# A recurrence and a two-layer network in FP32: the second group's second layer in three passes, a pair of blocks begun one group later

## The chip, the cores and the metric

The kernel runs on one core of a Trainium2 chip. A core has engines that run side by side, each with an instruction queue of its own: TensorE (PE: matrix products, with weight loads as a queue beside them), VectorE (DVE), ScalarE (ACT), GpSimd (POOL), and SyncE (SP), which here issues every DMA transfer. The metric is the device time of one execution in microseconds (us), as a median of several runs.

## The reference: what is computed

First a gated recurrence, for 4 batches and 8 heads of 48 numbers over 768 steps:

```
state = alpha[t][:, None] * state + outer(k[t], v[t])
y[t]  = q[t] @ state
```

Then y, seen as x of 3072 tokens by 384 numbers, goes through a network with two weight matrices (384 x 2048 and 2048 x 384):

```
h = max(x @ w_in, 0);  out = (h * h) @ w_out
```

All results are FP32.

## The kernel before

**Attention.** The 3072 tokens are 24 blocks of 128. A block's recurrence is computed by sums of logs (`cs`, lines 297 to 301), exponentials of them that scale q and k, transposes (`turn`, line 590, tile T), products of scores and state sums (`sckv`, lines 432 and 460), a masked copy (`am`, line 443), a new state (`us` and `s`, lines 473, 489, 490; the last factor comes by a DMA round trip, `last<-row`, line 344) and the outputs (`y`, line 412), which ScalarE copies into x (line 628). Blocks are taken in pairs, named by the first block: pair 12 is blocks 12 and 13. The function `attention` lists a pair's steps with due times. A call begins one pair (`n0`) and, with `after`, also finishes the pair before it; then the products sckv of the new pair and y of the old one share two interruptions of the network's products (`ga` and `gb`).

**Network.** Four blocks make a group, six groups in all (g = 0 to 5; the text calls g = 1 the second group and g = 2 the third). The weights are eight pieces per matrix, and a piece makes two of the sixteen 128-wide tiles of h. The first group uses true FP32 products ("plain"). From the second on a number is split into a near part a (or b for a weight), a rest l and a difference d, and a product of two numbers becomes three single passes: near by near, rest by rest, difference by difference. The first layer is `in_x` (the first two passes) and `in_y` (the third, two tiles later), line 737; `in_post` squares the result. The second layer is `out_x` and `out_y`, both through `of_tile`, line 820. In the second layer the first group has six plain pieces (`out_plain`) and two in three passes, the second group four and four (k1 = 4), and the others have all eight in three passes.

**Splits.** `split_h` makes ha on ScalarE (line 710) and hl on VectorE (line 660), `diff_h` makes hd on VectorE (line 714). The weights are prepared once, in the first and second group: `cast_w` (line 665, ScalarE), `rest_w` (line 660, VectorE), `scale_w` (line 679, ScalarE) and `diff_w` (line 660, VectorE). Rests and differences are stored to DRAM (`keep`, line 670) and read again for each later group (`pump`, line 703). `pump` reads ahead only while the number of pieces held is under `room`. The near parts stay.

**Order of work.** The network's steps are units with planned costs (1.05 for `in_x`, 1.08 for `out_x`). Everything else is an event with a due time in the same units, and `weave` puts the events between the units; each engine then runs its instructions in that order. All due times are in the table `AT`. `align` (line 1018) is an event too: it pads TensorE's instruction stream with NOPs up to a given offset within 256 instructions; `pads` gives group, time and offset, and `places` the pair ahead of whose transposes one stands.

Of the kernel before, what the change touches and what calls it, by code (L numbers as in the profile page):

```python
# [18 lines left out]
AT = {'v_by': (2.5, 3.5, 5.0), 'before': 2.2, 'places': ((4, 203), (16, 188)), 'pads': ((1, 33.0, 218), (2, 0.5, 83), (2, 5.5, 178)), 'evs': 0.65, 'lead': 4, 'post': 3, 'w_first': (45.25, 42.0, 55.95), 'wstep': 1.6, 'w_in_at': 2.5, 'w_late': 0.6, 'w_in_by': 3.4, 'room1': 22, 'room': 25, 's0': 4, 'ahead': 6, 'late': 2, 'xs': 0.2, 'g0': ((1.5, 4, False, True, 28.25), (20.25, 6, True, True), (28.75, 8, True, False)), 'sc0': (2.35, 2.35, 2.35), 'g1': ((5.5, 8, False, 15.5), (15.5, 10, True), (34.5, 12, True)), 'g': ((1.7, 6, True), (15.5, 8, True)), 'g1x': 50.0, 'gx': 48.25, 'g0x': 55.25, 'k0': 2, 'h0': 16, 'k1': 4, 'h1': 3, 'h1by': 2, 'evs0': 0.3, 'tp': 'ADMD', 'tp1': 'ADAD', 'split': 8, 'o0': (44.75, 47.25), 'o1': (), 'o2': (21.75, 27.5, 31.75, 35.0, 41.25, 41.75), 'str1': 22.0, 'ga': 9.5, 'gb': 13.0, 'cv0': 1.5, 'first': 'ln0 warm0 cs0 load0v load2a ei0 load1v eb0 mk0 ln1 fill1 fill1 kT0 cs1 kc0 eb1 mq0 qT0 mq1 ei1 qc0 fill1 mk1 fill1 lt0 sc0 lt1 kT1 kv0 qT1 am0 ln2 weights2 us0 load2q kc1 qc1 cs2 sc1 fill1 am1 load2k ei2 load3a eb2 load4a fill1 kv1 st0 first0 us1 fill1 middle0 ln3 mq2 load3k ya0 qT2 yb0 mk2 fill1 qc2 kT2 cs3 kc2 load3q load2v weights5 sc2 eb3 load3v fill1 sga0 sgb0 fill1 ei3 ev0 mq3 mk3 am2 fill1 late0 qT3 kT3 sgc0 first1 kc3 qc3 middle1 kv2 ha0 sc3 us2 kv3 sga1 ha1 am3 us3 sgb1 load4k ya2 load4q load4v first2 yb2 late0 sgc1 middle2 weights6 ev2 lt3 lt2 st2 ha3 ha2 sgb2 sga2 hb1 sgc2 hb0 hb2 weights1 st1 hb3 st3 weights0'}  # L19
# [6 lines left out]
def kernel(  # L26
# [640 lines left out]
    made, stored, cut = {}, set(), set()  # L667

    def keep(x, w, p):
        nc.sync.dma_start(out=kept_parts[x, w, p], in_=words(made[x, w, p]))  # L670
        stored.add((x, w, p))

    def rest_w(w, p):
        l = made["l", w, p] = wt("wl", FP32R, shapes[w])
        combine(((l, whole[w][p], ALU.subtract, here["b", w, p].bitcast(FP32)),))

    def scale_w(w, p):
        l = made["l", w, p]
        nc.scalar.activation(out=l, in_=l.bitcast(FP32), func=AF.Copy, scale=1.0 / E)  # L679
        keep("l", w, p)  # L680

    def diff_w(w, p):
        b, l = here["b", w, p].bitcast(FP32), made["l", w, p].bitcast(FP32)
        d = made["d", w, p] = wt("wd", FP32R, shapes[w])
        cut.add((w, p))
        combine(((d, b, ALU.subtract, l),))
        keep("d", w, p)
        for x in "ld":
            t = made.pop((x, w, p))
            if w == "i" or p >= NW - AT["k0"] or (x == "l" and p >= NW - AT["k1"]):  # L690
                here[x, w, p] = t
        pump()

    def prepare(at, w, p, late=0):
        step = AT["wstep"]
        fs = (cast_w, rest_w, scale_w, diff_w)
        return [(at + i * step + late * (i > 1), f, (w, p)) for i, f in enumerate(fs)]

    def pump():
        while todo and todo[0] in stored and len(here) + len(made) + 2 * NW - len(cut) < room[0]:  # L700
            key = todo.pop(0)
            here[key] = wt("w" + key[0], FP32R, shapes[key[1]])
            nc.sync.dma_start(out=words(here[key]), in_=kept_parts[key])

    def used(*key):
        here.pop(key)
        pump()

    def split_to(a, l, x):
        nc.scalar.activation(out=a, in_=x, func=AF.Copy, scale=NEAR)  # L710
        combine(((l, x, ALU.subtract, a.bitcast(FP32)),))

    def diff_to(d, a, l):
        nc.vector.scalar_tensor_tensor(
            out=d, in0=a.bitcast(FP32), scalar=-E, in1=l.bitcast(FP32), op0=ALU.mult, op1=ALU.add
        )
# [45 lines left out]
    kinds = [""]  # L762
# [19 lines left out]

    def layer_in(g):
        units = []
        for n in range(NJ + 2):
            if n < NJ:
                units.append((1.05, in_x, (n,)))
            if 0 <= n - 2 < NJ:
                units.append((0.53, in_y, (n - 2,)))
            if 0 <= n - AT["post"] < NJ:  # L790
                units.append((0, in_post, (n - AT["post"],)))
            if AT["lead"] <= n < AT["lead"] + AHEAD and (g > 1 or AT["k1"] == NW):
                units += splits_of_h(0, n - AT["lead"])
# [22 lines left out]
    def splits_of_h(first, i):  # L816
        return [(0, split_h, (first + i, i)), (0, diff_h, (first + i,))]
# [18 lines left out]
    def out_plain(p, t, pieces):  # L836
# [3 lines left out]
        for n in (2 * p, 2 * p + 1):  # L840
            of_tile(t, hid[n], w_out[p][:, n % 2], start=n == 0, stop=n == 2 * pieces - 1)
        if p == pieces - 1:
            nc.scalar.activation(out=new_out(t), in_=acc.pop(t)[:, 0:DM], func=AF.Copy)

    def out_x(n, first):
        p, jj = divmod(n, 2)
        a, l = h_parts.pop(n)
        for t in range(GB):
            if n == first:
                new_sum(t)  # L850
            of_tile(t, a, here["b", "o", p][:, jj], start=n == first)
            of_tile(t, l, here["l", "o", p][:, jj], stop=n == NJ - 1)
            if n == NJ - 1:
                x = acc[t][:, 0:DM]
                if first:
# [25 lines left out]
    def layer_out(g):  # L881
        posts = [(0, in_post, (n,)) for n in range(NJ + 2 - AT["post"], NJ)] if g else []
        plain = NW - AT["k0"] if g == 0 else NW - AT["k1"] if g == 1 else 0
        first = 2 * plain
        units = [(1, out_plain, (p, t, plain)) for p in range(plain) for t in range(GB)]
        if plain:
            for i, x in enumerate(posts):
                units.insert(1 + 2 * i, x)
            posts = []
        if plain == NW:  # L890
            for t in range(GB):
                units.append((0, lambda t: store(g, t, out_tile(t)), (t,)))
            return units
        ahead = AT["ahead"]
        split = [f for i in range(0 if plain else AHEAD, NJ - first) for f in splits_of_h(first, i)]
        if g == 0:
            split = [f for i in range(NJ - first) for f in [(0, split_h, (first + i, 0)), (0, diff_h, (first + i,))]]
        if plain:
            at = AT["h0" if g == 0 else "h1"]
            for i in range(min(AHEAD, len(split) // 2)):  # L900
# [5 lines left out]
        for n in range(first, NJ):  # L906
            units.append((1.08, out_x, (n, first)))
            if posts:
                units.append(posts.pop(0))
            while split and NJ - (len(split) + 1) // 2 <= n + ahead and (  # L910
                split[0][1] is diff_h or split[0][2][1] - AHEAD - MORE <= n - first
            ):
                units += [split.pop(0), split.pop(0)]
        ps = list(range(plain, NW))
        steps = [ps] if g == NG - 1 else [ps[i : i + 2] for i in range(0, len(ps), 2)]
        for pair in steps:
# [28 lines left out]

    def ffn_out(g, t, i):
        per = NJ // NW
        if i == 0:
            acc[t] = ps_ffn.tile([128, GB * C], FP32, tag="att", name="o")
        for j in range(per):  # L950
            nc.tensor.matmul(
                out=acc[t][:, 0:DM],
                lhsT=hid[per * i + j][:, t * C : (t + 1) * C],
                rhs=w_out[i][:, j, :],
                start=(i == 0 and j == 0), stop=(i == NW - 1 and j == per - 1),
            )
        if i == NW - 1:
            if t % 2 == 0:
                acc["out", t // 2] = cv_pool.tile([128, 2, DM], FP32, tag="upper", name="osb")
            o = acc["out", t // 2][:, t % 2, :]  # L960
            nc.scalar.activation(out=o, in_=acc.pop(t)[:, 0:DM], func=AF.Copy)
            store(g, t, o)
# [115 lines left out]
    def plain_out(g):  # L1078
        n = NW - AT["late"]
        units = [(1, ffn_out, (g, t, i)) for i in range(n) for t in range(GB)]  # L1080
        return units + [(1, ffn_out, (g, t, i)) for t in range(GB) for i in range(n, NW)]

# [8 lines left out]
    def begun(g):  # L1091
        kinds[0] = AT["tp1" if g == 1 else "tp"]
        room[0] = AT["room1" if g == 1 else "room"]

    def stream(g):
# [7 lines left out]
        stream_out(NW)  # L1103

    def stream_out(n, xs="ld"):
        todo.extend((x, "o", p) for x in xs for p in range(NW - n, NW))
        pump()
# [9 lines left out]
    units += layer_out(0) if AT["k0"] else plain_out(0)  # L1117
# [6 lines left out]
    for p, at in enumerate(AT["w_first"]):  # L1124
# [62 lines left out]
```

## Time and profile before

| | |
|---|---|
| median of 3 runs | 520.86 us (520.27 to 522.01) |
| the profiled execution | 521.61 us, of it span 519.8 us |
| granted TensorE clock | 1.000 |
| second group, first layer | 126.3 to 166.5 us |
| second group, second layer | 166.5 to 214.8 us |
| third group | 214.8 to 295.6 us |

The span goes from the first to the last instruction; the rest of the execution's time lies outside it. Weight loads are an engine of their own in the profile (PEld). A line such as "o<-wl,hl" names the tile written and the tiles read. A matrix product's record shows its whole way through the array (0.33 us for 384 columns in one pass), while the next one starts behind it sooner; so a product's price is taken from start to start, or from a long run in the chain.

### The profile page before, as it was taken

How to read it: one execution, taken by the hardware profiler on the slowest of the kernel's cores; microseconds unless marked ns; L12 is line 12 of the kernel's file. 1: busy time of each engine (PE TensorE's matmuls, PEld its weight loads, DVE VectorE, ACT ScalarE, POOL GpSimd, SP SyncE). 2: the span in 40 equal slices, each digit the busy share in tenths (PEclk: the TensorE clock that was granted, in tenths of full speed). 3: DMA queues.
4: the chain of work that ended last, by engine and by line, in shares of the span. 5: the costliest groups of instructions: out<-in, count | busy, mean ns of one | idle time of the engine just before them, and what ended most of it. 6: DMA issues, size and time to landing. Idle time of an engine off the chain costs nothing.

```text
span 519.8 us, 13204 instructions
## 1 busy us (share of the span) xinstructions
PE 511.1 (98%) x5350; PEld 421.5 (81%) x5350; DVE 361.9 (70%) x629; ACT 316.4 (61%) x664; POOL 5.4 (1%) x29
## 2 busy tenths in 40 slices
PE   8989999999999999999999999999999999999997
PEld 6775446668887669888899988899988899988997
DVE  3887969998979579757596466696465485363861
ACT  5678893687899566476963266962266863164620
POOL 4000000000000000000000000000000000000000
PEclk9999999999999999999999999999999999999999
DMA  9999686517878496998885796965684534798101
GB/s 182 210 262 262 178 216 172 75 51 240 243 228 200 117 280 161 272 338 234 201 235 156 242 269 185 231 172 162 217 269 124 183 123 153 254 355 295 68 0 62
DMA packets 139324, 102.36 MB, mean 197 GB/s; under 512 B 109808, under 2 KB 112896, under 8 KB 139264
## 3 DMA queue, kind: packets, MB, share of 16 engines
q1 hardware_dynamic: 139264, 101.52, 68.6%
q8 instruction: 43, 0.70, 0.6%
q14 instruction: 17, 0.14, 0.1%
HBM read 84.17 MB, written 17.33 MB: 195 GB/s over the span
## 4 chain that ended last, share of the span: by engine, by line
PE 93%; DVE 3%; DMA 1%; SPq 1%; issue 1%; ACT 0%; DVEq 0%; POOLq 0%
PE o L820 41%; PE h L737 32%; PE h L930 8%; PE y L412 4%; PE T L590 2%; PE sckv L432 2%; PE sckv L460 2%; DVE x L628 1%; DMA a_in<-in_alpha_dram 1%; PE cs L297 1%; SPq L344 1%; DMA last<-row 1%; PE cs L301 1%; PE cs L300 1%; SPq L119 0%
## 5 line engine op out<-in xcount | busy, mean ns | idle before, releaser
L737 PE MATMUL h<-xa,wb 128*128 128x512 f32 x240 | 69.2, 396 | 1.2 <-PE h L737 0.8
L737 PE MATMUL h<-xl,wl 128*128 128x512 f32 x240 | 68.1, 392 | 0.0
L737 PE MATMUL h<-xd,wd 128*128 128x512 f32 x240 | 66.6, 393 | 0.0
L754 ACT ACTIVATE h<-h 128x512 f32<-128x512 f32 x40 | 23.3, 581 | 57.9 <-PE h L737 57.7
L660 DVE TENSOR_TENSOR hid<-h,hid 128x512 f32<-128x512 f32 x40 | 27.5, 688 | 42.1 <-PE h L737 39.3
L628 ACT COPY x<-y 32x256 f32<-32x256 f32 (+2 forms) x132 | 47.2, 365 | 15.7 <-PE y L412 13.2
L820 PE MATMUL o<-wb,ha 128*128 128x384 f32 x160 | 54.2, 339 | 0.0
L820 PE MATMUL o<-wd,hd 128*128 128x384 f32 x304 | 53.7, 334 | 0.0
L820 PE MATMUL o<-w_out,hid 128*128 128x384 f32 x160 | 53.5, 490 | 0.0
L820 PE MATMUL o<-wl,hl 128*128 128x384 f32 x160 | 53.5, 334 | 0.0
L737 PEld LDWEIGHTS h<-xl,wl 128*128 128x128 f32 x240 | 44.9, 188 | 10.6 <-ACT wl L679 0.6
L737 PEld LDWEIGHTS h<-xa,wb 128*128 128x128 f32 x240 | 44.2, 188 | 11.1 <-PE h L737 1.2
L820 PEld LDWEIGHTS o<-wd,hd 128*128 128x128 f32 x304 | 52.8, 188 | 0.0
L737 PEld LDWEIGHTS h<-xd,wd 128*128 128x128 f32 x240 | 44.5, 188 | 9.2 <-ACT hid L752 0.2
L820 PE MATMUL o<-wb,hx 128*128 128x384 f32 x144 | 48.7, 338 | 0.0
L820 PE MATMUL o<-wl,hx 128*128 128x384 f32 x144 | 48.1, 334 | 0.0
L820 PEld LDWEIGHTS o<-w_out,hid 128*128 128x128 f32 x160 | 29.9, 190 | 19.7
L930 PE MATMUL h<-x,w_in 128*128 128x512 f32 (+1 forms) x120 | 43.0, 510 | 1.5 <-DVE s L489 1.2
L710 ACT ACTIVATE ha<-hid 128x512 fp32r<-128x512 f32 x40 | 25.4, 636 | 23.8 <-DVE hx L660 12.9
L752 ACT ACTIVATE hid<-h 128x512 f32<-128x512 f32 x40 | 24.3, 607 | 25.1 <-PE h L737 25.0
L930 PEld LDWEIGHTS h<-x,w_in 128*128 128x128 f32 x120 | 22.5, 190 | 18.6 <-issue 14.9
L660 DVE TENSOR_TENSOR hl<-hid,ha 128x512 fp32r<-128x512 f32 x40 | 27.4, 685 | 10.9 <-ACT ha L710 10.8
(115 smaller groups left out, 883.0 us busy)
## 6 DMA issues: line engine op xcount, KB each, us to landing
wd<-do SPq DMA_DIRECT2D x36, 384.0 KB
wl<-lo SPq DMA_DIRECT2D x34, 384.0 KB
wl<-li SPq DMA_DIRECT2D x32, 384.0 KB
wd<-di SPq DMA_DIRECT2D x32, 384.0 KB
raw<-in_moe_w_in_dram SPq DMA_DIRECT2D x8, 768.0 KB
raw<-in_moe_w_out_dram SPq DMA_DIRECT2D x8, 768.0 KB
v_in<-in_v_dram SPq DMA_DIRECT2D x24, 192.0 KB
out_dram<-osb SPq DMA_DIRECT2D x24, 192.0 KB
```

The lines of the kernel that those rows point to most:

```text
L412: ins = nc.tensor.matmul(out=ys[e][64 * half : 64 * half + D + G * e, m % 2, p // 2, t], lhsT=lhsT, rhs=rhs, start=(half, e) not in seen, ...
L432: nc.tensor.matmul(out=ps[e][HALF[h], 0, p, :], lhsT=ks[rows, p, HALF[h]], rhs=qs[rows, p, HALF[h]], start=True, stop=True, skip_group_che ...
L460: nc.tensor.matmul(out=ps[h][64 * e : 64 * (e + 1), 1, p, G:64], lhsT=tile_of("k", n)[HALF[h], 2 * p + e, :], rhs=tiles["v"][n % NV][HALF[ ...
L590: nc.tensor.transpose(out=ps[h][:, i, p, :], in_=rows[HALF[h], 128 * p : 128 * (p + 1)], identity=ident[HALF[h], HALF[h]],)
L628: copy(out=x[kk][to : to + m, t : t + 2], in_=blk[n]["y"][e][r : r + m, :, p // 2],)
L660: nc.vector.tensor_tensor(out=o, in0=x, in1=z, op=op)
L710: nc.scalar.activation(out=a, in_=x, func=AF.Copy, scale=NEAR)
L737: nc.tensor.matmul(out=acc["h", j], lhsT=here[w, "i", p][:, kk, jj * 128 : (jj + 1) * 128], rhs=x_parts[x][:, kk], start=start and kk == 0 ...
L752: nc.scalar.activation(out=hid[j], in_=x, func=AF.Copy, scale=E)
L754: nc.scalar.activation(out=x, in_=x, func=AF.Copy, scale=1.0 + E)
L820: nc.tensor.matmul(out=acc[t][:, 0:DM], lhsT=lhs[:, t * C : (t + 1) * C], rhs=rhs, start=start, stop=stop, skip_group_check=True,)
L930: nc.tensor.matmul(out=ps, lhsT=w[:, kk, c0 : c0 + 128], rhs=xT[g][kk][:, cols], start=(kk == 0), stop=(kk == KM - 1),)
```

## The change

- The second group's second layer has all eight pieces in three passes. It takes the pieces in the order 6, 7, 0 to 5, in both layers; its first three tiles are split during the first layer (`lead1`).
- For pieces 0 to 5 of `w_out` the rest stays in its buffer through the second group, and the difference is written over it, late: due at 39.99 units into the group and every 0.4 after. It was a step of 1.6 units behind the scaling, in a buffer of its own.
- The near parts carry a minus sign, so subtractions become additions and the reverse.
- Pair 12 is begun in the third group; in the second group the third call only finishes pair 10. The third group has three calls of its own (`g2`).
- Splits of h are listed 3 units ahead of their use instead of 6, in all groups.
- Pads: the description counts 98 NOPs.
- Unused functions go.

Of the table `AT`, beside smaller shifts of due times:

| entry | before | after |
|---|---|---|
| g1 | (5.5, 8), (15.5, 10), (34.5, 12) | (2.88, 8), (15.62, 10), (30.48, finish 10 only) |
| third group | (1.7, 14), (15.5, 16) | (2.31, 12), (19.24, 14), (32.13, 16) |
| o2 (casts of six pieces) | 21.75, 27.5, 31.75, 35.0, 41.25, 41.75 | 21.87, 23.25, 26.75, 27.38, 29.86, 36.12 |
| w_in_at, w_in_by | 2.5, 3.4 | 0.23, 3.9 |
| g1x (split of the next x) | 50.0 | 47.87 |
| room1, str1, ahead | 22, 22.0, 6 | 23, 25.88, 3 |
| pads (group, time, offset) | (1, 33.0, 218), (2, 0.5, 83), (2, 5.5, 178) | (1, 19.5, 15), (2, 6.0, 107), (2, 20.0, 95), (2, 40.5, 52) |
| places | (4, 203), (16, 188) | (4, 198), (16, 172) |

```diff
+    def lasting(w, p):
+        return w == "o" and p < NW - AT["k0"]
...
-        nc.scalar.activation(out=b, in_=whole[w][p], func=AF.Copy, scale=NEAR)
+        nc.scalar.activation(out=b, in_=whole[w][p], func=AF.Copy, scale=-NEAR)
...
     def rest_w(w, p):
-        l = made["l", w, p] = wt("wl", FP32R, shapes[w])
-        combine(((l, whole[w][p], ALU.subtract, here["b", w, p].bitcast(FP32)),))
+        l = here["l", w, p] = wt("wl", FP32R, shapes[w])
+        combine(((l, whole[w][p], ALU.add, here["b", w, p].bitcast(FP32)),))
...
     def diff_w(w, p):
-        b, l = here["b", w, p].bitcast(FP32), made["l", w, p].bitcast(FP32)
-        d = made["d", w, p] = wt("wd", FP32R, shapes[w])
-        cut.add((w, p))
-        combine(((d, b, ALU.subtract, l),))
+        l = here["l", w, p]
+        d = here["d", w, p] = here.pop(("l", w, p)) if lasting(w, p) else wt("wd", FP32R, shapes[w])
+        combine(((d, here["b", w, p].bitcast(FP32), ALU.add, l.bitcast(FP32)),))
         keep("d", w, p)
...
     def pump():
-        while todo and todo[0] in stored and len(here) + len(made) + 2 * NW - len(cut) < room[0]:
+        while todo and todo[0] in stored and len(here) + 2 * NW - len(cut) < room[0]:
...
-    def used(*key):
-        here.pop(key)
+    def used(x, w, p):
+        if g_now[0] != 1 or x != "l" or not lasting(w, p):
+            here.pop((x, w, p))
         pump()
...
+    def pieces(g):
+        last = [*range(NW - AT["k0"], NW)]
+        return last if g == 0 else last + [*range(NW - AT["k0"])] if g == 1 else [*range(NW)]
...
     def layer_out(g):
-        plain = NW - AT["k0"] if g == 0 else NW - AT["k1"] if g == 1 else 0
+        ps, ns = pieces(g), tiles_of(g)
+        plain = NW - len(ps)
...
-            for t, n0, after, *other in AT["g1"] if g == 1 else AT["g"]:
+            for t, n0, after, run, *other in AT["g1"] if g == 1 else AT["g2"] if g == 2 else AT["g"]:
...
-            for i, at in enumerate(AT["o1"] + AT["o2"]):
-                events += prepare(at0 + at, "o", order[len(AT["o0"]) + i])
+            for i, at in enumerate(AT["o2"]):
+                events += prepare(
+                    at0 + at, "o", order[len(AT["o0"]) + i], 0, at0 + AT["d_at"] + AT["d_by"] * i
+                )
```

More of the change, by code (lines that the diff above doesn't have):

```diff
@@ L840, in out_plain, with out_x @@
         for n in (2 * p, 2 * p + 1):
-            of_tile(t, hid[n], w_out[p][:, n % 2], start=n == 0, stop=n == 2 * pieces - 1)
-        if p == pieces - 1:
+            of_tile(t, hid[n], w_out[p][:, n % 2], start=n == 0, stop=n == 2 * end - 1)
+        if p == end - 1:
             nc.scalar.activation(out=new_out(t), in_=acc.pop(t)[:, 0:DM], func=AF.Copy)
-    def out_x(n, first):
+    def out_x(n, ns):
         p, jj = divmod(n, 2)
@@ L944, in store @@
         nc.sync.dma_start(out=out[r0 : r0 + C, :], in_=o)
[L946 to L962, printed above, removed]
     steps = {f.__name__: f for f in (ln, sp, cs, eb, ei, mq, mk, bl, br, lt, qT, qc, kT, kc, ev)}
```

127 lines of the change are left out of this document (56 added, 71 removed).

## The prediction

> **What bounds the kernel now.** I read the page first: engine shares, then the chain that ended last. TensorE is busy for 98% of the span at full granted clock and carries 93% of the chain, so time is won only by giving it less to stream or by taking away its few waits.
>
> ```profile
> PE 511.1 (98%) x5350; PEld 421.5 (81%) x5350; DVE 361.9 (70%) x629; ACT 316.4 (61%) x664; POOL 5.4 (1%) x29
> ...
> PE 93%; DVE 3%; DMA 1%; SPq 1%; issue 1%; ACT 0%; DVEq 0%; POOLq 0%
> ```
>
> Second view: the chain in order of time, for the price of the two kinds of second-layer product.
>
> ```profile
> 175.93 10.52 PE o L820 x32
> ...
> 216.18 0.80 issue
> ...
> 421.00 29.32 PE o L820 x168
> ```
>
> The first line lies in the second group's plain stage: 32 records are 16 plain products (two records each), so one costs 10.52 / 16 = 0.658 us. The last line is nothing but single passes, 29.32 / 168 = 0.1745 us each; three of them make 0.524 us. The middle line is a hole of 0.80 us behind the first six products of the third group.
>
> Third view: TensorE's waits in total, of which I use these two.
>
> ```profile
> PE h L737 <- PE h L737: 0.8, 1, 0.8
> PE h L737 <- DVE hid L660: 0.4, 1, 0.4
> ```
>
> "PE waits for PE" is no real wait. The instructions of line 1018 (the pads) show what it is: 158 NOPs in five runs of 58, 26, 26, 26 and 22, and one run of 26 stands at 215.0 to 216.9 us. It ends just where the next product starts (216.97). So one NOP costs TensorE's sequencer about 1.9 / 26 = 0.07 us, hidden where the sequencer is ahead of the array, and here it was not.
>
> Fourth view: the second group in two halves (first layer, then second), and the third group.
>
> ```profile
> 126.30:166.50 40.20, 40.20 (x349) 31.75 (x347) 35.64 (x63) 35.37 (x72) 0.00 (x0) 1.00 0.73 203
> 166.50:214.80 48.30, 48.30 (x710) 38.44 (x710) 38.23 (x70) 30.51 (x67) 0.00 (x0) 1.00 0.75 205
> 214.80:295.60 80.80, 79.61 (x921) 71.17 (x921) 52.67 (x99) 45.46 (x103) 0.00 (x0) 1.00 0.81 236
> ```
>
> The columns are the length, then busy time of TensorE, weight loads, VectorE and ScalarE. In the second group TensorE never rests, but VectorE (35.64 of 40.20) and ScalarE (35.37) are close behind it in the first layer. That is where the change adds work.
>
> **The change, part by part**, against the profiled execution (521.61 us, span 519.8, 1.8 outside); the median of the runs is 520.86, 0.75 lower, and the sum is carried to it.
>
> *Four pieces from plain to three passes.* 4 pieces x 2 tiles x 4 blocks = 32 products, from 0.658 to 0.524 us: 32 x 0.134 = **-4.3 us**, all on the path. The Trainium skill ("FP8 and Floating Point Precision", "TensorE Precision Notes") counts a true FP32 product as four passes; by that three passes would save a quarter of 0.658, 5.3 us in all. The rows give 4.3: the measured ratio is 0.80, not 0.75.
>
> *The pair moved.* Pair 12 is begun in the third group: its cs (4 x 0.18), T (1.15) and sckv (2 x 1.08), 4.0 us of TensorE, go from one group to the next at no change of the sum. But y of pair 10 was done in the same two breaks as sckv of pair 12, and now each has its own: two breaks more. A break costs the product before it 0.10 us (0.27 from start to start instead of 0.17, at 420.03), about 0.12 in the attention's own products and 0.11 in the first product after it (0.28, at 420.93), so 0.33: **+0.65 us** (0 to 0.9).
>
> *Pads.* 158 NOPs become 98, and the pad at 0.5 units into the third group goes (its first there is now at 6.0). The hole of 0.80 goes: **-0.8** (0 if another run is bare: 98 x 0.07 is 6.9 us of sequencer time, so +2 for one bare run of 26). I take -0.8 since four of the five runs of now cost nothing visible. The same skill ("Runtime: NRT & Kernel Launch", "Instruction fetch mechanics") says that instructions come in blocks of 256 and that crossing into one is mostly hidden; by that the pads themselves can only cost, and the sum stays the same. No row shows a hole at such a crossing.
>
> *VectorE and ScalarE.* Eight more tiles are split: on ScalarE 8 x 0.636 (ha) = 5.1 us, on VectorE 8 x (0.685 + 0.692) = 11.0. Out go pair 12 (VectorE 7.9: twice hi and lo 0.91, k and q 1.10, am 0.88, us 0.35, s 0.71; ScalarE about 6.2) and the four scaled adds of line 857 (2.2). The six differences of 0.95 only move to the end. Net +0.9 on VectorE and -1.1 on ScalarE, in a group that gets 8.3 us shorter (4.3 + 4.0): 74.8 busy of 80.2, 93% instead of 83%. By halves: the first layer gets three splits, 35.64 + 4.1 = 39.8 of 40.2; the second has 38.23 + 6.9 - 7.9 - 2.2 = 35.0 of 40.0.
>
> What is late next? The third group has the second layer in just the new form. There the last hl (VectorE) ends at 280.8 and TensorE reaches that tile at 282.8: 2.0 us to spare. The second group has four of its rests (0.95 each) in the same stretch, -3.8, and y of pair 10 (1.4 and its break) ahead of the last tile on TensorE, +1.7: 0.1 us short. With one wait of the kind now at 241 us (0.4) this makes **+0.55**. The bounds are 0 and what rival 1 gives.
>
> *Edits at nothing.* The signs: subtract and add on VectorE stand at the same 0.685 (hl and hid, 512 wide). Differences in the rests' buffers: on VectorE 0.95 as now. Each waits for TensorE's last product on its rest, a new wait; behind it on VectorE stand the other differences (5.7 us in all), the next x's parts (3.8) and the last adds, all under the output's difference passes, 4 x 16 x 0.1745 = 11.2 us. The first pair of them, 2.8 us, needs no new difference. If VectorE comes there late, TensorE waits by as much. Differences are stored later, six transfers of 384 KB on SP's queue in front of the third group's rests (rival 2). The third group takes pair 12's 7.9 us on VectorE: 52.67 + 7.9 = 60.6 of about 84; if that cover is gone it costs a wait like the 0.4. The pair's loads (eight transfers of 192 KB) and its round trip last<-row move with it on SP's queue; 1.6 MB in 84 us are 19 GB/s beside 236. Splits three units ahead instead of six change only the order in which VectorE and ScalarE take them; in groups 3 to 6 the spare 2.0 us covers it. Earlier loads and weights in groups 1 and 2: both queues carry the same transfers.
>
> Sum: -4.3 + 0.65 - 0.8 + 0.55 = **-3.9 us**, so 517.7 for the profiled execution and **517.0** by the median.
>
> **Rivals.**
> 1. *VectorE and ScalarE become the bound in the second group's first layer* (the one that ends on the other side). From 133 to 148 us ScalarE is busy 14.91 of 15.00 and VectorE 12.36, and just there (fifth to seventh tile) three splits come in. A tile's ScalarE step must be done before its third pass, 3.4 us after its first two (1.39 + 0.68 + 1.39); the step takes 0.58 and is now some 1.0 late, so 1.8 us of lag are free, and the splits add 1.9 on ScalarE and 4.1 on VectorE. For it: these rows. Against it: VectorE's idle time there is mostly waiting for ScalarE (2.5 at 146 us), which lag swallows, and pair 8 and the weights come in earlier. If all of the first half's 4.6 us of idle stay, the layer is 39.8 + 4.6 - 40.2 = 4.2 longer, 521.2; if the second half's 10.1 stay too, another 5.1 (35.0 + 10.1 - 40.0), 526.3. It decides from 3.9 us of lag on: beyond that slower than now, beyond 5.5 measurably.
> 2. *The third group's reloads are late.* Now the first rests are issued at 207.9, 6.9 us before the group. Then the buffers are held until the first pair of difference passes ends, 8.4 us before it, but behind six stores. 2.36 MB at the 306 GB/s of 208 to 213 us take 7.7 us and are done in time; at the group's mean of 204 GB/s they and three reloads (3.5 MB) take 17 us from about 13 before the start, 4 late, with 1 to 3 felt: 518 to 520. SP takes its queue in order, so a late sixth difference on VectorE holds the reloads behind it.
> 3. *The passes gain and nothing waits*: -4.3 - 0.8 - 0.4 (the wait at 241) and breaks at 0: 515.4.
> 4. *The plain products' time doesn't go* (single passes at a slower pace between mixed attention work): the third group shows them at full pace in the same mix, so I give it no share of its own.
>
> **How the numbers follow.** Forecast with small waits 0.60 (515.5 to 518.6); rival 1 between 518.6 and 522.4 0.17, above it 0.10; rival 2 0.08; rival 3 0.05. A difference under 0.3% (1.56 us) can't be told from none here, so faster means below 519.3: 0.60 + 0.05 + 0.04 + half of rival 2 and a little of rival 1 make 0.74; above 522.4 0.11; between 0.15. The range goes from 514.5 (rival 3 with 0.9 for the spread of the runs) to 520.8, which leaves out rival 1's upper part and some of its middle, not quite 0.2.
>
> **What would show it.** Right: no record of plain products between 160 and 215 us, the second group about 8 us shorter, the third about 4 longer, no hole of 0.8 behind its first products. Wrong: TensorE waiting in the second group for hid, ha or hx (rival 1), for wl or wd at the third group's start (rival 2), or a run of NOPs that ends at the start of a product. The forecast fails if VectorE in the first layer falls more than 4 us behind.

## The result and the profile after

In 20 executions of each on the same chip the kernel after took 521.96 us (521.34 to 523.46) and the kernel before 521.24 (520.13 to 522.08): a ratio of 1.0016 [1.0009, 1.0024]. The forecast was 517.0, a gain of 3.9; there is none, the kernel after is 0.7 us slower. The profiled execution took 522.13 us, 520.4 of it span, against 521.61 and 519.8.

The page of after, engine shares and the chain that ended last:

```profile
PE 509.7 (98%) x5382; PEld 427.0 (82%) x5382; DVE 371.0 (71%) x641; ACT 321.0 (62%) x672; POOL 5.3 (1%) x29
...
PE 91%; DVE 4%; DMA 3%; ACT 2%; issue 0%; SPq 0%; DVEq 0%; ACTq 0%
```

TensorE is busy 1.4 us less than before, and yet its share of the chain fell by two points. In the second group, where the chain of before stays on TensorE, that of after leaves it twice: from 135.2 to 140.5 us, which costs TensorE less than 0.3 us, and from 175.9 to 185.6 us, over ScalarE and VectorE. Of TensorE's waits on others in after (engine, line, who ended them: us in total, times, longest) these lie in second layers, line 833, the last of them in the third group:

```profile
PE o L833 <- ACT ha L714: 1.6, 1, 1.6
...
PE o L833 <- DVE hl L660: 0.8, 2, 0.5
...
PE o L833 <- DVE hx L660: 0.3, 1, 0.3
```

In after, line 741 is the first layer's product (737 before), 833 the second's (820), 714 makes ha, 660 the rests, 718 the differences of h, 671 casts a weight and 685 scales its rest. Lengths of the stages, in the profiled executions, from a layer's first product to the next layer's first, in us (the attention's break ahead of the second group's second layer, from 166.5 us in before, so counts to the first layer here):

| stage | before | after | measured | forecast |
|---|---|---|---|---|
| start and first group | 126.26 | 126.81 | +0.55 | 0 |
| second group, first layer | 42.70 | 42.58 | -0.12 | 0 |
| second group, second layer | 45.66 | 40.98 | -4.68 | -7.75 |
| third group | 80.98 | 85.44 | +4.46 | +3.85 |
| fourth to sixth | 220.77 | 220.97 | +0.20 | 0 |
| sum | | | +0.41 | -3.9 |

So 3.1 of the 4.3 us that are missing lie in one stage. The windows show it: length, then busy time of TensorE, weight loads, VectorE and ScalarE. First the second group's second layer in before:

```profile
168.96:214.62 45.66, 45.66 (x552) 35.87 (x550) 36.09 (x65) 28.08 (x63) 0.00 (x0) 1.00 0.73 203
```

Then, in after, the second group's first layer, its second layer, and the third group:

```profile
126.81:169.39 42.58, 42.36 (x505) 34.82 (x505) 40.65 (x72) 39.09 (x79) 0.00 (x0) 1.00 0.73 205
169.39:210.37 40.98, 38.62 (x420) 36.79 (x418) 33.40 (x54) 25.75 (x54) 0.00 (x0) 1.00 0.67 208
210.37:295.81 85.44, 85.02 (x1086) 75.21 (x1086) 59.16 (x115) 50.02 (x117) 0.00 (x0) 1.00 0.78 216
```

The first layer, where I feared VectorE and ScalarE, runs with them at 95 and 92% and TensorE at its pace. In the second, TensorE is busy 38.62 of 40.98; in before it never rested there. The timeline of TensorE there (start, length, in brackets the idle time and who ended it):

```profile
180.81 0.34 PE L833 MATMUL o<-wl,hx 128*128 128x384 f32 x1
182.71 0.44 PE L833 MATMUL o<-wb,ha 128*128 128x384 f32 x1 [1.56 <-ACT ha L714]
183.43 0.44 PE L833 MATMUL o<-wl,hl 128*128 128x384 f32 x1 [0.28 <-DVE hl L660]
...
185.63 0.44 PE L833 MATMUL o<-wl,hl 128*128 128x384 f32 x1 [0.52 <-DVE hl L660]
```

From start to start the three steps take 1.90, 0.72 and 0.85 us instead of 0.174: 2.95 us, from the eighth of the 16 tiles on. ScalarE's timeline says why ha was late:

```profile
172.12 1.57 ACT L671 ACTIVATE wb<-w_out 128x768 fp32r<-128x768 f32 x2
175.92 2.17 ACT L628 COPY x<-y 32x256 f32<-32x256 f32 x6 [2.23 <-PE y L412]
177.99 0.84 ACT L671 ACTIVATE wb<-w_out 128x768 fp32r<-128x768 f32 x1
178.84 1.14 ACT L628 COPY x<-y 32x256 f32<-32x256 f32 x3
180.01 0.85 ACT L685 ACTIVATE wl<-wl 128x768 fp32r<-128x768 f32 x1
180.88 1.13 ACT L628 COPY x<-y 64x256 f32<-64x256 f32 x3
182.03 0.63 ACT L714 ACTIVATE ha<-hid 128x512 fp32r<-128x512 f32 x1
```

ScalarE takes its queue in order. It stood idle for 2.23 us at a copy of y into x that waited for TensorE's y, and then worked through 12 copies, a cast and a scaling before it came to the split. That split was for the very next tile: TensorE had caught up. VectorE, behind it, idled for 2.00 us for the same ha.

### The profile page after: what moved, and what is told of

Read it like the earlier page. It is cut to its first block, busy times and chain, and to the rows that moved or that the text cites. A ratio compares the mean times of both kernels' runs of the same rounds, so it can differ in the third digit from the quotient of the medians.

```text
span 520.4 us, 13203 instructions
## 1 busy us (share of the span) xinstructions
PE 509.7 (98%) x5382; PEld 427.0 (82%) x5382; DVE 371.0 (71%) x641; ACT 321.0 (62%) x672; POOL 5.3 (1%) x29
## 4 chain that ended last, share of the span: by engine, by line
PE 91%; DVE 4%; DMA 3%; ACT 2%; issue 0%; SPq 0%; DVEq 0%; ACTq 0%
PE o L833 38%; PE h L741 31%; PE h L933 7%; PE y L412 4%; PE sckv L432 2%; PE T L590 2%; PE sckv L460 2%; DMA raw<-in_moe_w_in_dram 1%; ACT x L628 1%; DMA a_in<-in_alpha_dram 1%; PE cs L297 1%; PE zeros L398 1%; DMA wd<-do 1%; DVE x L628 0%; PE cs L300 0%; PE cs L301 0%
## 5 line engine op out<-in xcount | busy, mean ns | idle before, releaser
L833 PE MATMUL o<-wb,ha 128*128 128x384 f32 x176 | 60.2, 342 | 1.6 <-ACT ha L714 1.6
L833 PE MATMUL o<-wl,hl 128*128 128x384 f32 x176 | 59.4, 338 | 0.8 <-DVE hl L660 0.8
L660 DVE TENSOR_TENSOR hid<-h,hid 128x512 f32<-128x512 f32 x40 | 27.5, 689 | 42.4 <-PE h L741 42.4
L833 PE MATMUL o<-wl,hx 128*128 128x384 f32 x160 | 53.8, 336 | 0.4 <-DVE hx L660 0.3
L833 PE MATMUL o<-wb,hx 128*128 128x384 f32 x160 | 54.2, 338 | 0.0
L833 PE MATMUL o<-wd,hd 128*128 128x384 f32 x288 | 51.6, 335 | 0.0
L833 PEld LDWEIGHTS o<-wd,hd 128*128 128x128 f32 x288 | 49.9, 188 | 0.2
L660 DVE TENSOR_TENSOR hl<-hid,ha 128x512 fp32r<-128x512 f32 x44 | 30.2, 687 | 15.3 <-ACT ha L714 15.1
L714 ACT ACTIVATE ha<-hid 128x512 fp32r<-128x512 f32 x44 | 27.8, 641 | 13.0 <-DVE hx L660 5.4
L833 PEld LDWEIGHTS o<-wb,ha 128*128 128x128 f32 x176 | 33.0, 188 | 2.6 <-ACT ha L714 1.9
L833 PEld LDWEIGHTS o<-wl,hl 128*128 128x128 f32 x176 | 33.0, 188 | 2.2 <-DVE hl L660 1.8
```

Source lines behind the costliest of these rows:

```text
L660: nc.vector.tensor_tensor(out=o, in0=x, in1=z, op=op)
L714: nc.scalar.activation(out=a, in_=x, func=AF.Copy, scale=-NEAR)
L833: nc.tensor.matmul(out=acc[t][:, 0:DM], lhsT=lhs[:, t * C : (t + 1) * C], rhs=rhs, start=start, stop=stop, skip_group_check=True,)
```

## The experiments

Ratios are against the kernel before, run beside each one on the same chip. Three theories stood in turn. The *order*: ScalarE and VectorE have time enough, and the splits, three units ahead, come too late in their queues. The *load*: in any order the two have too much to do between 170 and 200 us. After the first runs a third, *both stacked*: with three ahead ScalarE's order holds a tile back; with six ahead VectorE has no gap left, and the last piece's rest comes late instead.

### Order, pair and pad

`a_ahead6`: after, with the old look-ahead.

```diff
-'ahead': 3
+'ahead': 6
```

> The changed kernel with splits of h listed 6 units ahead of their use, as before the change, instead of 3. Theory 1 (order): in the second group's second layer the split of the eighth tile stands on ScalarE behind the twelve copies of y and the weights' casts and scales, because it is listed only 3 units ahead; TensorE then waits 1.6 us for ha and 0.8 for hl there, and 0.8 in the same way for hx at 270 us. Listed 6 ahead, the waits go: 3 to 5 us less than the changed kernel, 517 to 518.5 us, ratio to before 0.993 to 0.996. Theory 2 (load): ScalarE and VectorE simply lack time in that stage; the wait moves to another tile, hx or wl, and the time stays at 520.5 or more (ratio 0.999 to 1.003).

1.0043 [1.0027, 1.0058], 523.61 us. The wait for ha is gone, and yet the second group's second layer is 42.75 us long, 1.8 more than in after: TensorE now waits for a scaled rest. Of the 1.8, 1.3 come from nine passes behind that wait, which start 0.32 us apart instead of 0.1735, at a lower granted clock (more at the end). The waits alone are 3.0 us from start to start, as in after. TensorE's timeline, then VectorE's, then ScalarE's:

```profile
194.10 0.45 PE L833 MATMUL o<-wb,ha 128*128 128x384 f32 x1
196.33 0.45 PE L833 MATMUL o<-wl,hl 128*128 128x384 f32 x1 [1.78 <-ACT wl L685]
```

```profile
193.12 0.69 DVE L660 TENSOR_TENSOR hl<-hid,ha 128x512 fp32r<-128x512 f32 x1
193.84 0.69 DVE L718 SCALAR_TENSOR_TENSOR hd<-ha,hl 128x512 fp32r<-128x512 f32 x1
194.45 0.95 DVE L660 TENSOR_TENSOR wl<-w_out,wb 128x768 fp32r<-128x768 f32 x1
```

```profile
189.96 0.83 ACT L671 ACTIVATE wb<-w_out 128x768 fp32r<-128x768 f32 x1
195.44 0.84 ACT L685 ACTIVATE wl<-wl 128x768 fp32r<-128x768 f32 x1 [4.65 <-DVE wl L660]
```

The last piece's cast is done at 190.8; its rest starts only at 194.45, behind splits and differences, and the differences are needed only at the layer's end. VectorE's busy time from 171.4 to 199.8 us is 27.26 of 28.40. The order alone is not it.

`a_copies_late`: after, with the copies of y that stood in front of ha put later.

```diff
-out.append((w + AT["evs" if scale == 1 else "evs0"] * p, ev_part, (old, p)))
+out.append((w + {10: 5.0, 14: 3.0}.get(n0, 0) + AT["evs" if scale == 1 else "evs0"] * p, ev_part, (old, p)))
```

> The changed kernel with the copies of y into x due 5 units later in the second group (pair 8) and 3 units later in the third (pair 12); splits still listed 3 units ahead. Theory 1: the splits now stand ahead of the copies, so the waits for ha and hl at 181 to 186 us go as they do with the longer look-ahead: 2 to 4 us less than the changed kernel, ratio 0.994 to 0.998. Theory 2: the copies' 4.4 us on ScalarE are still needed in the same stage and a later tile waits: ratio 0.999 to 1.003. If the output sums then wait for a free bank, the time is above the changed kernel's.

1.0031 [1.0019, 1.0042], 523.24 us. The wait for ha is gone, which shows that the copies made it. In its place stand, in the second group, 1.4 us for hl and 0.9 for hx, and in the third 0.7 for hx and 0.3 for hl; the two second layers are 41.51 and 48.07 us, against 40.98 and 47.21.

`a_pair_back`: after, with pair 12 begun in the second group again.

```diff
-'g1': ((2.88, 8, False, True, 15.62), (15.62, 10, True, True), (30.48, 12, True, False))
+'g1': ((2.88, 8, False, True, 15.62), (15.62, 10, True, True), (30.48, 12, True, True))
-'g2': ((2.31, 12, False, True), (19.24, 14, True, True), (32.13, 16, True, True))
+'g2': ((1.96, 14, True, True), (15.38, 16, True, True))
```

> The changed kernel with pair 12 begun in the second group again (in the third call, at its due time of 30.48), and the third group's calls back at 1.96 and 15.38. Two breaks of TensorE's stream fewer (-0.65 us) and the third group's second layer free of a second pair, so its waits for hx (0.8) go; the second group gets 7.9 us of VectorE and 6.2 of ScalarE in its second layer. Theory 1: the wait at 181 stays as it is (the pair's steps come after it), so 0 to 2 us less than the changed kernel, ratio 0.998 to 1.002. Theory 2: the second group's second layer gets longer by most of the added work, 3 us or more above the changed kernel, ratio above 1.006.

1.0831 [1.0800, 1.0862], 564.2 us. As a whole it answers nothing: the offsets of the pads stayed, the instructions ahead of them did not, and there are three runs of 194, 255 and 103 NOPs; TensorE waits 32.1 us for "issue". The second group lies ahead of them. Its second layer is 48.33 us, 7.35 longer, with 2.4 us for ha and 1.4 for T; the pair's own products are 3.9 of it. So with three ahead the pair costs 3.4 us more there than its products. With the edits found below it was not tried there.

`b_pad_late`: before, with the pads of the third group moved into its middle.

```diff
-'pads': ((1, 33.0, 218), (2, 0.5, 83), (2, 5.5, 178))
+'pads': ((1, 33.0, 218), (2, 20.0, 83), (2, 25.0, 178))
```

> The kernel before, with the two pads of 26 NOPs in the third group at 20.0 and 25.0 units instead of 0.5 and 5.5; nothing else. If the hole of 0.80 us behind the third group's first six products is the sequencer passing the pad, it goes: 0.8 us less, ratio 0.998 to 0.999. If the hole is the wait for the first reloaded rest, it stays and the ratio is 1.000. Against both: other instruction addresses could make a hole elsewhere, ratio above 1.001.

1.0828 [1.0810, 1.0845], 565.5 us, for the same reason: 477 NOPs in place of 158, in runs of up to 225 (252.0 to 268.6 us) and 168 (from 283.8 us). The waits of TensorE, "issue" being time in which the profile shows nothing that it waits for:

```profile
PE h L737 <- issue: 15.2, 2, 14.4
PE o L820 <- issue: 12.1, 1, 12.1
PE y L412 <- issue: 9.4, 3, 3.5
```

The 225 NOPs leave TensorE without a product for 14.4. 16.6 / 225 is 0.07 us for one, the price that the prediction had from 26 of them. The line of y is not a pad; more on it at the end.

### Load

`a_pool_rest`: after, six rests of weights made on GpSimd.

```diff
-        combine(((l, whole[w][p], ALU.add, here["b", w, p].bitcast(FP32)),))
+        x, b = whole[w][p], here["b", w, p].bitcast(FP32)
+        if lasting(w, p):
+            nc.gpsimd.tensor_tensor(out=l, in0=x, in1=b, op=ALU.add)
+        else:
+            combine(((l, x, ALU.add, b),))
```

> The changed kernel with the rests of the six late pieces of w_out (4 of the 6 fall into the second group's second layer) computed by GpSimd, which is otherwise idle, instead of VectorE; the result is the same. Theory 2, VectorE's share: the 0.95 us each that VectorE is spared let the splits catch up, so most of the 3.5 us lost in that layer come back: 2 to 3.5 us less than the changed kernel, ratio 0.995 to 0.998. Theory 2, ScalarE's share: the splits' near parts wait behind copies, casts and scalings on ScalarE; no gain, ratio 1.000 to 1.003. If GpSimd takes several us for a piece, the scaled rest comes late and TensorE waits for wl: above 1.003.

1.0055 [1.0037, 1.0072], 523.6 us. The group of GpSimd's instructions (count, then busy us and mean ns), and VectorE's timeline beside two of them:

```profile
L683 POOL TENSOR_TENSOR wl<-w_out,wb 128x768 fp32r<-128x768 f32 x6 | 13.5, 2251 | 171.2 <-ACT wb L671 171.2
```

```profile
173.43 0.69 DVE L660 TENSOR_TENSOR hx<-hid,hx 128x512 fp32r<-128x512 f32 x1
174.16 2.20 DVE L722 SCALAR_TENSOR_TENSOR hd<-hx 128x512 fp32r<-128x512 f32 x1
176.28 2.31 DVE L660 TENSOR_TENSOR hx<-hid,hx 128x512 fp32r<-128x512 f32 x1
```

GpSimd takes 2.25 us where VectorE took 0.95, and VectorE's own 0.69 become 2.2 and 2.3 beside it. VectorE got no relief; the waits are 1.5 us (ha) and 1.6 (hl). The Trainium skill ("SBUF — State Buffer", "SBUF: two separate sides") says that a VectorE step with two inputs in SBUF and a GpSimd step that reads SBUF take one pair of ports in turn, an instruction at a time. The trace agrees: 2.2 is about one GpSimd instruction. On the load this run answers nothing.

`a_zero_rest`: the same six rests, but the work on VectorE left out.

```diff
...
+        if lasting(w, p):
+            nc.gpsimd.memset(l.bitcast(FP32), 0.0)
+        else:
+            combine(((l, x, ALU.add, b),))
```

> The changed kernel with the rests of the same six pieces not computed: GpSimd sets them to zero early, and VectorE's six steps are left out. This is the upper bound of the run with GpSimd's rests: VectorE's share of theory 2 says 3 to 4 us less than the changed kernel (ratio 0.993 to 0.996), ScalarE's share says no gain (1.000 to 1.002).

1.0022 [1.0010, 1.0034], 522.41 us. With 5.7 us of VectorE's work gone, the second layer is 40.17 us, 0.8 shorter than in after, and ha's 1.6 us stay. (That the median is not below that of after is a matter of the granted clock, at the end.) The load alone is not it either.

`a_pool_scale`: after, six scalings from ScalarE to GpSimd.

```diff
+        if lasting(w, p):
+            nc.gpsimd.tensor_scalar(out=l, in0=l.bitcast(FP32), scalar1=1.0 / E, scalar2=None, op0=ALU.mult)
...
```

> The changed kernel with the scaling of the rests of the same six pieces on GpSimd instead of ScalarE (0.84 us each). ScalarE's share of theory 2: the near part of the eighth tile comes up to 2.5 us earlier, the wait of 1.6 us for ha goes, 1.5 to 3 us less than the changed kernel, ratio 0.995 to 0.999. VectorE's share: the wait moves to hl, no gain, 1.000 to 1.003.

1.0038 [1.0026, 1.0050], 523.17 us. ha waits 0.6 instead of 1.6, hl 1.4, and 0.6 go to the scaling on GpSimd (2.34 us each); the layer is 41.92 us.

`b_pad_covered`: before, without the pad at 0.5; its 26 NOPs go into the second group's pad.

```diff
-'pads': ((1, 33.0, 218), (2, 0.5, 83), (2, 5.5, 178))
+'pads': ((1, 33.0, 244), (2, 5.5, 178))
```

> The kernel before, with the pad at 0.5 units into the third group left out and its 26 NOPs added to the pad in the second group's plain stage (52 there, where TensorE's sequencer was 3 us ahead of the array behind the NOPs); all instructions behind the old pad keep their place in their block of 256. If the hole of 0.80 us is the pad, it goes: 0.8 us less, ratio 0.998 to 0.999. If it is the reloaded rest's arrival, 1.000.

1.0000 [0.9991, 1.0008], 521.03 us. Its four runs of NOPs have 22 to 58. In its profile the hole of 0.8 us is gone and the third group 1.5 shorter, the second group's second layer 0.6 longer, and the time is the same.

### Both stacked

`a6_zero`: six ahead and the zeroed rests of `a_zero_rest` together.

```diff
-'ahead': 3
+'ahead': 6
...
+            nc.gpsimd.memset(l.bitcast(FP32), 0.0)
```

> The changed kernel with both: splits listed 6 units ahead, and the rests of the six late pieces of w_out set to zero by GpSimd instead of computed on VectorE. Theory 3 (two bounds stacked): with the short look-ahead ScalarE's order holds the eighth tile back (so sparing VectorE brought 0.8 us alone), with the long one VectorE is busy without a gap from 171 to 199 us (so the order alone brought nothing); only both together free TensorE. The second group's second layer then takes 37.5 to 38.5 us (41.0 in the changed kernel, 42.8 with the long look-ahead alone), total 2 to 3 us less than the changed kernel, ratio 0.995 to 0.999. Theory 1 and theory 2 in ScalarE's form: 40 us or more there, ratio 1.001 or more. The third group's wait for cs stays in either.

0.9969 [0.9958, 0.9980], 519.70 us. Neither half helped by more than 0.8 us; together they take 3.2 off the second layer: 37.77 us, with no wait of TensorE in it. The stacked theory gave this; the order alone and the load alone did not.

`a_hd2`: after (`ahead` 3), with the differences of h two tiles later on VectorE.

```diff
-            split += [(0, split_h, (ns[i], 0 if g == 0 else i)), (0, diff_h, (ns[i],))]
+            split.append((0, split_h, (ns[i], 0 if g == 0 else i)))
+            m = i - 2 if g == 1 else i
+            split.append((0, diff_h, (ns[m],)) if m >= (0 if plain else AHEAD) else (0, lambda: None, ()))
...
```

> The changed kernel with the differences of h in the second group listed two tiles later than their splits, so that on VectorE the next rest (hl, hx) goes ahead of them; same work, same look-ahead of 3. If VectorE's order is what makes hl late, the waits for hl (0.8 us) go, ratio 0.999 to 1.001; the wait of 1.6 us for ha stays, as it is ScalarE's. Theory 1 alone: no change from the changed kernel (1.001 to 1.002).

1.0017 [1.0005, 1.0030], 522.15 us: nothing. The longer of the two waits for hl goes, but ha's 1.6 us stay, so ScalarE's order binds as long as the look-ahead is three. The layer is 41.73 us in the profiled execution, since ten passes behind the wait for ha start 0.32 us apart.

`a6_hd3o`: all of the work kept; six ahead, the differences of h three tiles later, and the last piece earlier.

```diff
-'ahead': 3, 'o2': (21.87, 23.25, 26.75, 27.38, 29.86, 36.12)
+'ahead': 6, 'o2': (21.87, 23.25, 26.75, 27.38, 29.86, 34.0)
...
+            m = i - 3 if g == 1 else i
```

> The changed kernel with the splits listed 6 ahead, the differences of h in the second group three tiles late, and the last late piece's cast due at 34.0 instead of 36.12. Theory 3: the 2 us of differences that no longer stand ahead of the rests let VectorE meet TensorE; the waits for hx (0.5) and wl (1.8) go or shrink under 0.5, and with them the lower clock behind them. The second group's second layer 38 to 39.5 us, ratio 0.998 to 1.001. If VectorE lacks time altogether, the wait only moves: 41 us or more, ratio above 1.002.

0.9968 [0.9956, 0.9981], 519.43 us, and the same 37.77 us without a wait as with the work left out. So the load fits. VectorE is nearly as busy as in `a_ahead6`, 26.00 us of the same 28.40, but TensorE never rests:

```profile
171.40:199.80 28.40, 28.40 (x364) 27.46 (x363) 26.00 (x41) 19.98 (x42) 0.00 (x0) 1.00 0.63 197
```

VectorE's timeline of this kernel at the end of the layer: the last piece's rest starts 20.73 us into the layer, against 24.67 in `a_ahead6`, and what TensorE needs last, the differences, comes last.

```profile
189.55 0.95 DVE L660 TENSOR_TENSOR wl<-w_out,wb 128x768 fp32r<-128x768 f32 x1
190.42 0.69 DVE L660 TENSOR_TENSOR hl<-hid,ha 128x512 fp32r<-128x512 f32 x1
191.02 1.29 DVE L718 SCALAR_TENSOR_TENSOR hd<-hx 128x512 fp32r<-128x512 f32 x2
192.22 1.29 DVE L718 SCALAR_TENSOR_TENSOR hd<-ha,hl 128x512 fp32r<-128x512 f32 x2
193.43 5.30 DVE L660 TENSOR_TENSOR wl<-wb,wl 128x768 fp32r<-128x768 f32 x6
```

`b_ahead3`: before, with three ahead and nothing else.

```diff
-'ahead': 6
+'ahead': 3
```

> The kernel before with splits listed 3 units ahead instead of 6: the one part alone. My prediction priced it at nothing. If that holds, ratio 0.999 to 1.001 and the third group's second layer stays at 35.2 us; if it is this that costs the changed kernel its gain, the third group's second layer gets waits for ha or hx of 0.5 to 2 us, ratio 1.002 to 1.005.

0.9990 [0.9978, 1.0002], 520.75 us: where half the pieces are plain, three ahead costs nothing that can be told. The fifth group is 0.28 us longer, as in after. And its profile, with the pads of before, has no hole in the third group's first products: the pads alone don't make the hole of 0.8.

### Which of the two edits

`a6_hd3`: six ahead and the late differences, without the earlier last piece.

```diff
-'ahead': 3
+'ahead': 6
...
+            m = i - 3 if g == 1 else i
```

> The changed kernel with splits listed 6 ahead and the differences of h in the second group three tiles late; the last late piece is due at 36.12 as in the change. If the order of the differences is what cured the run with both edits: the second group's second layer 37.8 to 38.3 us, ratio 0.996 to 0.998. If it was the last piece's earlier due time: the wait of 1.8 us for wl stays, 40 us or more, ratio 1.001 or more.

1.0042 [1.0028, 1.0056], 523.32 us. The layer is 40.28 us, with one wait of 2.2 for the last piece's scaled rest. Its profiled execution (521.91 us) kept a mean clock of 1.000; eight of the twelve did not, and took 523.1 to 525.0.

`a6_o`: six ahead and the earlier last piece, differences as in the change.

```diff
-'ahead': 3, 'o2': (21.87, 23.25, 26.75, 27.38, 29.86, 36.12)
+'ahead': 6, 'o2': (21.87, 23.25, 26.75, 27.38, 29.86, 34.0)
```

> The changed kernel with splits listed 6 ahead and the last late piece's cast due at 34.0, the differences of h right behind their rests as in the change. If the due time alone cures the wait for wl: 38 to 39 us in that layer with waits for hx and hl of 0.5 to 1 left, ratio 0.998 to 1.000. If VectorE's order is what counts, the piece's rest goes ahead of the last splits and they come late instead: 39.5 us or more, ratio 1.000 to 1.004.

0.9996 [0.9985, 1.0006], 520.74 us; 38.91 us, 0.5 of wait for the same rest. From `a_ahead6`, 42.75, the earlier piece takes 3.8 and the late differences 2.5, but 1.3 of each is the lower clock in the profiled execution of `a_ahead6`. TensorE's waits, from start to start, go from 3.0 us to 0.9 and to 2.5; only both leave none and make 37.77. By the time of the runs the late differences alone bring nothing (1.0042 beside 1.0043).

`a6_hd3all`: `a6_hd3o` with the late differences in all groups after the first.

```diff
-            m = i - 3 if g == 1 else i
+            m = i - 3 if g else i
```

> The run with both edits, and the differences three tiles late in groups 3 to 6 as well. The third group's second layer holds a wait of 1.5 us of TensorE for cs of pair 16 (its hi and lo stand on VectorE behind splits) and 0.75 at its transposes. If that wait is again VectorE's order, the differences' 2 us that step back give it: third group's second layer 46.5 to 47.5 us instead of 48.4, total 1 to 2 us less than the run with both edits, ratio 0.993 to 0.996. If it is VectorE's load, the wait stays and the ratio is 0.996 to 0.998.

1.0001 [0.9990, 1.0012], 521.32 us. The second group keeps 37.77. The third group's second layer goes to 49.59 from 48.43: there the order delays q of a pair on VectorE, and T waits 1.9 us for it, with a lower clock behind. Eleven of its twelve executions have a mean clock of 0.996 or 0.997; the one with 0.999 took 519.47 us, no more than `a6_hd3o`.

### The third group, and a better version

With six ahead the third group's second layer is 48.43 us, with three 47.21. So the look-ahead was set by group.

`best_g2a3`: `a6_hd3o`, and in the third group three ahead.

```diff
-            while split and len(ns) - (len(split) + 1) // 2 <= i + AT["ahead"] and (
+            while split and len(ns) - (len(split) + 1) // 2 <= i + (3 if g == 2 else AT["ahead"]) and (
```

> The run with both edits of the second group (splits 6 ahead, differences three tiles late, last piece due at 34.0), and the third group back at splits 3 ahead as in the change. The third group's second layer took 47.2 us with 3 ahead in the changed kernel and 48.4 with 6: if the groups' waits are independent, 1.2 us less than the run with both edits, 518.2 us, ratio 0.993 to 0.996. If not, its wait for hx comes back larger, ratio 0.996 to 0.998.

0.9947 [0.9934, 0.9960], 518.16 us: faster than both kernels, by 3.0 us than before. Its page, and TensorE's waits in total:

```profile
PE 508.9 (99%) x5382; PEld 427.6 (83%) x5382; DVE 369.4 (72%) x641; ACT 321.1 (62%) x672; POOL 5.3 (1%) x29
```

```profile
PE h L939 <- DVE x L628: 1.1, 1, 1.1
PE warm L251 <- POOL s L67: 1.1, 1, 1.1
PE y L412 <- DVE us L473: 0.4, 1, 0.4
PE o L833 <- DVE hx L660: 0.3, 1, 0.3
```

The first three lie in the start and the first group. Only the last is left in the groups with three passes.

`best_g2a4`: four ahead in the third group. `best_g2turn`: `best_g2a3`, with pair 16's transposes due later and the pad ahead of them fitted. In one diff:

```diff
-i + (3 if g == 2 else AT["ahead"])
+i + (4 if g == 2 else AT["ahead"])
...
-(32.13, 16, True, True), 'places': ((4, 198), (16, 172))
+(32.13, 16, True, True, None, 39.7), 'places': ((4, 198), (16, 188))
```

> The same with the third group's splits 4 ahead: between the wait for hx (0.8 us with 3 ahead) and the waits for cs and T (2.2 us with 6 ahead). Ratio 0.992 to 0.997; under the one with 3 ahead if neither wait is whole.

> The run with the third group's splits 3 ahead, and pair 16's transposes due at 39.7 units of the group instead of 38.63, so that VectorE's scaled k and q are ready when TensorE gets there (the pad ahead of them keeps its run of 6 NOPs). The wait for q_in (0.3 us) and the copies between splits should go: 0.3 to 1 us less than with 3 ahead; if the pair's products then come late for the next group's x, a wait of 1 us or more at the fourth group's start.

0.9952 [0.9937, 0.9967], 518.56 us, not to be told from `best_g2a3`; and 0.9967 [0.9955, 0.9980], 519.46 us, with 1.4 us of wait for hx in place of 0.3. Every order tried in the third group leaves some wait there: hx with three ahead, T with four, cs (1.3 us) and T with six.

## Why the prediction was wrong

**The four pieces, -4.3: right.** In the second group's second layer 64 records of plain products with 20.74 us are gone. 96 passes more at 0.1735 are 16.66, so 4.1 are saved. Without waits the layer is 37.77 us, 7.9 less than before, against the planned 8.3 (4.3 and the pair's 4.0).

**What is late next, +0.55: this step failed.** It measured 3.2 (40.98 against 37.77). I took the margin of the third group's last tile on VectorE, 2.0 us, and corrected it by what VectorE gets. (The parts given for it, 0.1 and 0.4, make 0.5; and the margin was 2.5, since TensorE needs that hl at 283.29. Neither is what failed.) The wait came at the eighth tile, due at 181.0 us, and on ScalarE; the sixteenth begins at 197.05 and finds its hl done (196.03). The last tile's margin says nothing of an engine that takes its queue in order and stops at a copy that waits for TensorE. Rival 1 named the two engines and a wait for ha, but the first layer; that layer kept its time (42.58), just where I put the danger. That rival 1's time for it, 521.2, lies near the 521.96 measured is chance.

**Three units ahead, at nothing: wrong together with the step above.** I covered it by the same 2.0 us "in groups 3 to 6". Alone it costs nothing (`b_ahead3`). With the change it is one of two bounds on the second group's second layer; undone alone it lays the other one open, and TensorE waits as long as in after, 3.0 us, at other tiles (`a_ahead6`). That both have to go is shown by `a6_zero` and `a6_hd3o`. In the third group 0.52 and 0.30 us of waits for hx, from start to start, stand in after, and in the fifth 0.29 that `a_ahead6` takes back.

**The pair's two breaks, +0.65.** Third group: +4.46 is 4.0 for the pair, less 0.8 (the hole) and 0.4 (the wait at 241), plus 0.82 of new waits; 0.84 is left for the breaks. Inside its bounds of 0 to 0.9, and only a remainder.

**The pad, -0.8: not a gain to count on.** The 98 NOPs leave no hole in after. But `b_pad_covered` without the hole is no faster: 0.8 us would be a ratio of 0.9985, outside its interval. `b_ahead3` has no hole with the old pads. I took the hole of one execution for a term of the sum; whether it stands in every execution of before is open.

**Nothing for differences in the rests' buffers: right.** The six stand in a row, 5.29 us on VectorE, and no TensorE wait falls on them; rival 2's waits for reloads did not come.

**The rest.** Start and first group +0.55: in the profiled executions of before and its variants the second group begins at 126.3 to 127.3 us, in those of after and its variants at 125.9 to 127.2, so a difference of this size between two single executions can't be put down to the change. Added up, the misses are 3.1 in the second group's second layer, 0.6 in the third group, 0.55 at the start and 0.2 behind, less 0.1 in the first layer: 4.3, from -3.9 to +0.4. With the two bounds taken away, and three ahead kept in the third group (`best_g2a3`), the gain is 3.0 of the 3.9.

## What to carry to other kernels

When work leaves the engine that bounds a stage, walk the whole stage tile by tile and write down, for each helper engine, what stands ahead of each tile's step in its queue; a margin read at the last tile, or a share of busy time, misses an instruction that waits in the middle. Where undoing one suspect makes the kernel slower and undoing another does nothing, try both together before dropping either: two bounds can hide each other. And after moving instructions, count the NOPs of every alignment pad again, since a fixed offset turned 26 NOPs into 225 here.

## What the runs showed of the hardware

- **GpSimd and VectorE in turn.** In the second group's second layer of `a_pool_rest` four VectorE steps of 0.69 us took 2.1 to 2.3 beside the four GpSimd steps there (2.25 us on average), so each step moved cost VectorE more than the 0.95 it saved.
- **Transfers of instructions.** In `b_pad_late` TensorE's products of y stalled for 2.9 to 3.7 us, start to start, at three places with no pad, 235.0, 280.1 and 353.7 us. In each of these stalls a transfer of 16384 bytes of instructions runs (235.3 to 236.4, 281.4 to 282.3 and 354.8 to 355.8 us), and the products go on 1.3 to 1.5 us after its end. The Trainium skill ("Runtime: NRT & Kernel Launch", "Instruction fetch mechanics") calls the cost of crossing into a new block of 256 instructions mostly hidden. The trace of before has none of these stalls; in `b_pad_late` three were not hidden. The next transfer follows within 3.5 to 5.0 us, but in before two follow each other within 3.6 us (395.1 and 398.7) without a stall, so why these three stall is open.
- **The granted clock after a wait.** In `a_ahead6` the clock of the 4 us before TensorE's wait of 1.8 us is 1.00, and of 196 to 200 us, behind it, 0.62. In the profiled executions of `a_hd2` and after, the same wait of 1.6 us for ha is followed by ten passes at 0.32 us in the one and by none in the other; behind the 2.2 us in `a6_hd3` the clock stays at 1.00. So the length of the wait alone doesn't decide it. In `a_zero_rest` the executions with a mean clock of 1.000 took 521.1 to 521.6 us, and those with 0.997 took 522.4 to 523.5: there a wait costs over 1 us more than its own length. Six of the 20 executions of after have 0.997 as well. What decides whether the clock falls is open.
